# A fused FNet and GEGLU layer on one core: the opening of its pipeline in another order of instructions

## The chip, the core and the metric

The kernel runs on one core of a Trainium2 chip. The core has five engines with an instruction queue each: TensorE (PE in the profile, with its weight loads listed apart as PEld), VectorE (DVE), ScalarE (ACT), GpSimd (POOL) and SyncE (SP), which here only issues transfers. Each engine works through its own queue in order, and an instruction starts when what it waits for in other queues has come. The metric is the device time of one execution in microseconds (us); the median of three runs of the kernel before is 777.99 us.

## The reference, cut to what matters

`x` is 2048 rows by 448 columns. A normalised copy of it feeds two branches, and their product is added to `x`:

```
xn = layernorm(x)                                   # over the 448 columns
s  = dft_seq_re @ (xn @ dft_hid_re.T) - dft_seq_im @ (xn @ dft_hid_im.T)
g  = silu((gelu(xn @ w_gate) * (xn @ w_up)) @ w_down)   # w_gate, w_up 448x1792, w_down 1792x448
out = x + s * g
```

Everything is 32-bit. TensorE gets each operand as a rounded high part and a remainder, the low part; a product is high x high + high x low + low x high. So nearly every operand is made twice: ScalarE writes a high part (a copy to a rounded type), and VectorE or GpSimd subtracts it from the source to give the low part.

## The kernel before

The 2048 rows of `x` are four chunks c = 0 to 3 of 512 rows, each four tiles k of 128 rows. The 1792 columns of the two first weights are 14 blocks f of 128, in pairs; the work below on blocks 0 and 1 (the first pair) is the opening, some 75 us. After it come the other six pairs, in a Strassen form (`strassen`, L438 to L509) over two chunks at a time that needs differences of chunks and of weights; then the transforms. The first pair is done plainly so that TensorE has work while those differences are made.

The steps of the opening, with their lines before the change:

- `stats` gives four closures for a chunk. `one(i)` takes mean and variance of a tile (L155, L156, DVE). `root` takes a square root (L160, ACT) and two small terms (L161, L162); `newton` turns it into the reciprocal root in four DVE operations on 128 x 4 or 128 x 2 numbers (L166 to L170). `norm(i)` normalises a tile in place, on DVE in one operation (L178) or on ACT in two (L175, L176).
- `turn_mm` transposes a tile on TensorE into a PSUM bank (L187, two such banks in turn). `turn_split` then has ACT write the high part (L199) and one or two plain copies `xf` (L201), and DVE the low part (L202), in that order of writing.
- `prep_w` splits the raw weights of blocks 0 and 1: a high part, and a low part in two subtractions of 128 x 768 and 64 x 256 (L285, L287). Block 0 lies in `w`, block 1 in `wd`. In the kernel before GpSimd makes the low parts of block 0 and DVE those of block 1.
- `first` and `gu_mm` are the matmuls of gate and up (L556, L361). `act` runs the gelu of the gate on ACT (L386), and returns m (times up, DVE, L389), h (high part, ACT, L390) and l (low part, DVE, L391). ACT loads a table (ACT_TABLE_LOAD) when it goes from square root to gelu and back.
- `down_one` multiplies the result with the second weights (L415): for block 0 then block 1, the parts h, h and l, six matmuls in that order into one of two PSUM banks. ACT takes the result out (L422).
- `combine(p, s, eng)` are four subtractions of transposed tiles for a pair of chunks p and half s (L218, L222, L223, L224). The eight of chunks 0 and 1 are on DVE, put one by one between other steps (the list `comb`); the eight of chunks 2 and 3 are on GpSimd, and can start when the last copies of chunk 3 are there (GpSimd first clears a corner, L217).
- `prep_s` splits the weights of block 2 for the Strassen form, in two steps: ACT rounds (L321), DVE subtracts 128 x 512 and 64 x 384 in the first step and 128 x 896 in the second (L323, L327). `t_places` and `v_places` split the combined tiles (L143).

The scheduling is by hand (`tc.manual_schedule()`): each engine's queue is the order in which the Python code writes its instructions. `down` and `gateup` call closures from lists `between` and `between1` after each of their pieces, so that work of ACT and DVE falls between TensorE's.

Of the kernel before, what the change touches and what calls it, by code (L numbers as in the profile page):

```python
# [13 lines left out]
P = 128  # L14
# [31 lines left out]
def fnet_geglu(ctx: ExitStack, tc: tile.TileContext, x, ca, ct, cp, et, wgu, wd, out):  # L46
# [13 lines left out]
    nc = tc.nc  # L60
# [123 lines left out]
    def turn_mm(c, k):  # L184
        pt = tp_tile(f"pt{c}_{k}").rearrange("p (b d) -> p b d", b=4)
        for b in range(4):
            nc.tensor.transpose(pt[:, b], xr[c][:, k, b * P : (b + 1) * P], ident)  # L187
        return c, k, pt

    def turned(pt, c):  # L190
        return pt if c % 2 == 0 else pt.rearrange("p (b a) d -> p b a d", a=2)

    def cols_of(v, c, sl):
        return v[:, :, sl] if c % 2 == 0 else v[:, :, :, sl]

    def turn_split(c, k, pt):
        sl = slice(k * P, (k + 1) * P)
        h, l = [cols_of(xs(c, lo), c, sl) for lo in range(2)]
        nc.scalar.activation(h, turned(pt, c), AF.Copy)  # L199
        for i, v in enumerate(xf[c]):  # L200
            nc.scalar.activation(v[:, :, sl], pt[:, 3 * i :] if i else pt[:, : v.shape[1]], AF.Copy)  # L201
        nc.vector.tensor_sub(l, turned(pt, c), h)  # L202


    SPOT = ((0, 0), (1, 1), (1, 0), (0, 1))
# [310 lines left out]
    with tc.manual_schedule():  # L516
# [71 lines left out]
            nc.scalar.activation(xf[0][0][:, :, k * P : (k + 1) * P], t[2], AF.Copy)  # L588
        newton()
        norm(0)  # L590
        norm(1)
        ws[1][1](nc.vector)
        ws = [w[2] for w in ws]
        draw = load_d(GROUPS[0], a_r[0][:, 1024:])
        first(0, half[0], ("hh", "hl", "lh", "last"))
# [3 lines left out]
        one, root, newton, norm = stats(1, 0, 4)  # L599
        one(0)  # L600
        one(1)
        turn_split(*t2)
        turn_split(*t3)
        one(2)
        one(3)
        root()
# [8 lines left out]
        turn_split(*t0)  # L615
        turn_split(*t1)
# [4 lines left out]
        d_low()  # L621
# [5 lines left out]
        turn_split(*t2)  # L627
        turn_split(*t3)
        one(1)
        m0, h0, l0 = act(0, 0, pgs[0])  # L630
        m1, h1, l1 = act(1, 0, pgs[1])
        m0()
        h0()
        m1()
# [2 lines left out]
        one(3)  # L637
        root()
        l0()
        l1()  # L640
        newton()
        norm(0)
        norm(1)
        gu_mm(pg[0], ws[0], 0, 1, half[1], True)
        gu_mm(pg[1], ws[0], 1, 1, half[1])
        norm(2)
# [3 lines left out]
        pg = gu_ps(1, 1)  # L650
        for g in range(2):
            gu_mm(pg[g], ws[1], g, 1, slice(0, 512))
        turn_split(*turn_mm(2, 0))
        h0()
        xp = [dram.tile([P, 2, 1024], F32, name=f"xp{p}") for p in range(2)]

# [9 lines left out]
        spill(0)  # L666
        s_raw = load_s(GROUPS[1][0], 1)
        sums_s(s_raw, nc.gpsimd)
        comb = combine(0, 0, nc.vector) + combine(0, 1, nc.vector)

        def turn2(k):
            turn_split(*turn_mm(2, k))
            if k == 1:
                l0()
            comb.pop(0)()

        between = [lambda k=k: turn2(k) for k in (1, 2, 3)]
        down(0, 0, wdn, between)
# [1 line left out]
        one, root, newton, norm = stats(3, 0, 4)  # L680
        one(0)
        one(1)
        m1()
        h1()
        one(2)
        one(3)
        root()
        l1()
        newton()
        norm(0)  # L690
        norm(1)

        nws = [None, None]


        for c in (2, 3):
            if c == 2:
                draw = load_d(GROUPS[1], a_st[:, 2304:])
            else:
                s_raw2 = load_s(GROUPS[1][1], 1)  # L700
            m0, h0, l0 = gateup(0, c, ws[0])
            if c == 2:
                turn = lambda k: turn_split(*turn_mm(3, k))
                between = [
                    lambda: (m0(), h0(), norm(2)),
                    lambda: (l0(), norm(3), turn(0), comb.pop(0)()),
                    lambda: (turn(1), comb.pop(0)()),
                    lambda: (turn(2), comb.pop(0)()),
                ]
                between1 = [lambda: (turn(3), comb.pop(0)())]  # L710
            else:
                t_split = t_places(0)
                between = [
                    lambda: (m0(), v_split(2)),
                    lambda: (h0(), t_split(1)),
                    lambda: (l0(), t_split(2)),
                    lambda: (t_split(0), t_split(3)),
                ]
                between1 = [lambda: v_split(0), lambda: v_split(3)]
            down(0, c - 1, wdn, between)  # L720
            if c == 2:
                nws[0], steps = prep_s(0, s_raw)
                for f in steps:
                    f()
            m1, h1, l1 = gateup(1, c, ws[1], between1)
            m1()
            if c == 2:
                h1()
                l1()
                comb.pop(0)()  # L730
                v_split = v_places(0)
                v_split(1)
# [571 lines left out]
```

## Time and profile before

| | us |
|---|---|
| runs of the kernel before | 776.15, 777.99, 779.34 |
| median | 777.99 |
| profiled execution, its own time | 778.02 |
| span of the trace in it | 776.3 |
| granted TensorE clock over the span | 0.998 of full speed |

The profile is of one execution. A timeline row gives start, duration, engine, line and operation, tiles and shapes, and in brackets how long the engine stood idle before it and what ended that. Line numbers in rows are of the kernel before; in the changed file the same code stands 16 to 20 lines further down.

### The profile page before, as it was taken

What the parts mean: (1) busy time and instruction counts of PE and PEld (TensorE: products, weight loads), DVE (VectorE), ACT (ScalarE), POOL (GpSimd) and SP (SyncE); (2) the same over time, 40 slices, a digit from 0 to 9 for tenths busy, and PEclk for the clock granted to TensorE, in tenths of its full rate; (3) what the DMA queues carried; (4) which work ended last, traced back from release to release, by engine and by line L of the source; (5) the groups of instructions that cost most, each with busy time, mean ns of one, the idle gap of its engine ahead of it and who ended that gap; (6) DMA issues with size and microseconds to landing.
All of it is one profiled execution on the core that took longest, in us unless ns stands there. A gap on an engine that the chain in (4) does not pass through costs nothing.

```text
span 776.3 us, 11377 instructions
## 1 busy us (share of the span) xinstructions
PE 765.2 (99%) x4044; PEld 686.3 (88%) x4044; DVE 546.8 (70%) x937; ACT 363.6 (47%) x538; POOL 189.0 (24%) x308
## 2 busy tenths in 40 slices
PE   8999999999999999999999999999999999999997
PEld 7888888888888888888889999999999999899996
DVE  7789866555556555455553776988879696969687
ACT  3885545434434344344444685544344434434341
POOL 1109133330511512501011101223132231313120
PEclk9999999999999999999999999999999999999999
DMA  8232557994959968865979962869596969687784
GB/s 295 89 119 89 204 201 164 259 190 94 269 109 254 264 121 231 167 144 99 276 199 248 388 291 87 279 224 332 185 359 188 367 187 321 213 306 237 266 270 179
DMA packets 61370, 170.05 MB, mean 219 GB/s; under 512 B 7424, under 2 KB 40064, under 8 KB 60416
## 3 DMA queue, kind: packets, MB, share of 16 engines
q1 hardware_dynamic: 47440, 108.17, 39.4%
q0 software_dynamic: 13728, 61.02, 34.2%
q8 instruction: 32, 0.52, 0.3%
q14 instruction: 26, 0.21, 0.1%
q10 hardware_dynamic: 144, 0.11, 0.0%
HBM read 127.21 MB, written 70.91 MB: 255 GB/s over the span
## 4 chain that ended last, share of the span: by engine, by line
PE 83%; DVE 8%; DMA 5%; issue 2%; ACT 1%; SPq 0%; DVEq 0%; ACTq 0%
PE x L438 23%; PE po L415 17%; PE p L1111 16%; PE ab L927 9%; PE p L1114 8%; PE x L445 4%; PE gu L361 3%; DVE e L143 2%; DVE xt L143 1%; DMA raw<-wgu 1%; DMA raw_d<-ct 1%; DMA w<-td 1%; DMA raw<-ct 1%; DMA raw<-cp 1%; PE py L1126 1%
## 5 line engine op out<-in xcount | busy, mean ns | idle before, releaser
L438 PE MATMUL x<-xt,w 128*128 128x512 f32 x480 | 149.5, 392 | 0.0
L438 PEld LDWEIGHTS x<-xt,w 128*128 128x128 f32 x480 | 90.1, 188 | 16.1 <-DVE tmp L477 0.4
L422 ACT ACTIVATE po_out<-po 128x448 f32<-128x448 f32 x112 | 60.2, 538 | 82.1 <-PE po L415 81.2
L415 PE MATMUL po<-wd0h,hs 128*128 128x448 f32 x256 | 81.7, 366 | 0.0
L427 POOL DMA_DIRECT2D gs<-po_out x24 | 21.4, 890 | 219.3 <-ACT po_out L422 219.2
L927 PE MATMUL ab<-e,xt 128*128 128x448 f32 x288 | 68.8, 365 | 0.0
L415 PE MATMUL po<-wd,hs 128*128 128x448 f32 x288 | 66.0, 365 | 0.0
L438 PE MATMUL x<-t_v,w 128*128 128x512 f32 x216 | 60.7, 389 | 0.0
L415 PEld LDWEIGHTS po<-wd,hs 128*128 128x128 f32 x288 | 54.1, 188 | 6.7
L927 PEld LDWEIGHTS ab<-e,xt 128*128 128x128 f32 x288 | 54.1, 188 | 4.3
L415 PEld LDWEIGHTS po<-wd0h,hs 128*128 128x128 f32 x256 | 48.1, 188 | 5.0
L1006 POOL DMA_DIRECT2D raw<-sums x45 | 24.8, 551 | 98.4 <-DVE xt L143 30.6
L438 PEld LDWEIGHTS x<-t_v,w 128*128 128x128 f32 x216 | 40.5, 188 | 8.7
L415 PE MATMUL po<-wd0l,hs 128*128 128x448 f32 x128 | 46.9, 366 | 0.0
L142 ACT ACTIVATE e<-raw 128x896 fp32r<-128x896 f32 (+1 forms) x30 | 27.7, 922 | 34.3 <-DVE raw L1013 19.9
L493 ACT ACTIVATE hs<-tmp 128x512 fp32r<-128x512 f32 x24 | 15.2, 633 | 54.6 <-DVE tmp L491 54.6
L1111 PE MATMUL p<-t_v,wd0l 128*128 128x448 f32 x112 | 37.5, 380 | 2.8 <-DVE cc L1208 2.8
L438 PE MATMUL x<-t_lo,w 128*128 128x512 f32 x96 | 37.3, 389 | 0.0
L1006 POOL DMA_DIRECT2D tmp<-sums x39 | 21.4, 550 | 63.1 <-DVE xt L143 27.5
L1111 PE MATMUL p<-w,e 128*128 128x448 f32 x112 | 36.4, 374 | 0.0
L323 DVE TENSOR_TENSOR w<-raw,w 128x512 fp32r<-128x512 f32 (+1 forms) x24 | 21.3, 888 | 19.0 <-ACT w L321 19.0
L143 DVE TENSOR_TENSOR e<-raw,e 128x896 fp32r<-128x896 f32 (+1 forms) x30 | 31.4, 1046 | 4.4 <-ACT e L142 4.1
(317 smaller groups left out, 2015.5 us busy)
## 6 DMA issues: line engine op xcount, KB each, us to landing
gs<-po_out POOLq DMA_DIRECT2D x24, 896.0 KB, 8.3
sums<-ca SPq DMA_DIRECT2D x16, 896.0 KB, 9.8
sums<-ca POOLq DMA_DIRECT2D x16, 896.0 KB, 14.5
t_v<-td SPq DMA_DIRECT2D x24, 448.0 KB, 5.6
w<-td SPq DMA_DIRECT2D x24, 448.0 KB, 7.2
raw<-ct SPq DMA_DIRECT2D x45, 192.0 KB, 4.6
raw<-wgu SPq DMA_DIRECT2D x12, 640.0 KB, 5.7
tmp<-ct SPq DMA_DIRECT2D x39, 192.0 KB, 4.6
```

The costliest lines, as they stand in the source:

```text
L142: nc.scalar.activation(h, src, AF.Copy)
L143: nc.vector.tensor_sub(l, src, h)
L361: nc.tensor.matmul(ps[:, cols], a, xt[:, cols], start=n == 0, stop=n == len(mm) - 1)
L415: nc.tensor.matmul(po[:, :D], hs[:, a, kk * P : (kk + 1) * P], wdn[b][:, i], start=n == 0, stop=n == 5,)
L422: nc.scalar.activation(out_[0][:, kk], po[:, :D], AF.Copy)
L427: nc.gpsimd.dma_start(gv[:, 4 * c : 4 * c + 4], out_[0], accum_op=ALU.add)
L438: nc.tensor.matmul(ps, a[i], b[j], start=first and n == 0, stop=n == 2, skip_group_check=True)
L445: nc.tensor.matmul(ps, a[0], xt, start=False, stop=True, skip_group_check=True)
L927: nc.tensor.matmul(p[:, :D], a, b, start=n == 0, stop=n == len(mm) - 1)
L1006: nc.gpsimd.dma_start(v[:, 4 * P : 6 * P], sums[j][:, KS.index(k)])
L1111: nc.tensor.matmul(ps[q][:, :D], h, v, start=u % UN == 0, stop=False, skip_group_check=True)
L1114: nc.tensor.matmul(ps[q][:, :HD], l, v[:, :HD], start=False, stop=u % UN == NS - 1, skip_group_check=True,)
```

## The change

Seven edits, all in the opening:

1. `turn_split` takes several tiles. With two, it writes both high parts, then both low parts, then the copies; with one, the old order of low part after copies stays, unless `early` is set (set for tile 3 of chunk 2). `mid` is run between low parts and copies.
2. The second `norm` of tiles 2 and 3 of chunk 0 goes from DVE to ACT, and the low parts of block 1's weights go from DVE to GpSimd.
3. The gelus of chunk 0 (with their table load) are run ahead of the copies of chunk 1's last two tiles, and the low part of the second weights, `d_low`, after that pair's low parts.
4. l of block 1 (`l1`) of chunk 0 moves behind two norms of chunk 2.
5. Of the eight combinations of chunks 0 and 1, half 1 comes before half 0; the one at each tile of chunk 2 shrinks to one in all, and the others go to later places; three statistics of chunk 3 come before m of block 1, and l before the square root.
6. The gelu of block 0 of chunk 2, with its table load, moves from ahead of the second down to behind tile 2 of chunk 3; m, h and l with it.
7. The two steps of `prep_s` move from behind `down` (ahead of tile 3 of chunk 3) into the place between the two matmul groups of block 1: behind tile 3, between h, l of block 0.

```diff
+    def turn_split(*turns, mid=None, early=False):
+        hl = []
+        for c, k, pt in turns:
+            sl = slice(k * P, (k + 1) * P)
+            hl.append([cols_of(xs(c, lo), c, sl) for lo in range(2)])
+            nc.scalar.activation(hl[-1][0], turned(pt, c), AF.Copy)
+        def lows():
+            for (c, k, pt), (h, l) in zip(turns, hl):
+                nc.vector.tensor_sub(l, turned(pt, c), h)
+        early = early or len(turns) > 1
+        if early:
+            lows()
+        if mid:
+            mid()
+        for c, k, pt in turns:
...
+        if not early:
+            lows()
...
-        norm(1)
-        ws[1][1](nc.vector)
+        norm(1, nc.scalar)
+        ws[1][1](nc.gpsimd)
...
-        turn_split(*t2)
-        turn_split(*t3)
+        acts0 = []
+        turn_split(t2, t3, mid=lambda: acts0.extend(act(f, 0, pgs[f]) for f in range(2)))
+        d_low()
         one(1)
...
-        l1()
         newton()
         norm(0)
         norm(1)
+        l1()
...
-            turn_split(*turn_mm(2, k))
+            turn_split(turn_mm(2, k), early=k == 3)
             if k == 1:
                 l0()
-            comb.pop(0)()
+            if k == 1:
+                comb.pop(0)()
...
                 between = [
-                    lambda: (m0(), h0(), norm(2)),
-                    lambda: (l0(), norm(3), turn(0), comb.pop(0)()),
+                    lambda: norm(2),
+                    lambda: (norm(3), turn(0), comb.pop(0)()),
                     lambda: (turn(1), comb.pop(0)()),
-                    lambda: (turn(2), comb.pop(0)()),
+                    lambda: (turn(2), comb.pop(0)(), first.extend(act(0, 2, pg)), first[0]()),
                 ]
-                between1 = [lambda: (turn(3), comb.pop(0)())]
+                between1 = [lambda: (turn(3), first[1](), steps[0](), first[2](), steps[1]())]
...
                 nws[0], steps = prep_s(0, s_raw)
-                for f in steps:
-                    f()
             m1, h1, l1 = gateup(1, c, ws[1], between1)
             m1()
             if c == 2:
                 h1()
+                comb.pop(0)()
                 l1()
                 comb.pop(0)()
```

In VectorE's queue at the second statistics of chunk 0 (`sd_2`: two tiles) stood, before, the reciprocal root's steps, two norms, then the weights' low parts:

```order
L168 TENSOR_TENSOR sd_2_161<-sd_2_161 128x2
L169 TENSOR_TENSOR sd_2_161<-sd_2_161 128x2
L170 SCALAR_TENSOR_TENSOR sd_2_161<-sd_2_161 128x2
L178 TENSOR_SCALAR xr_a<-xr_a,mv_2_160,sd_2_161 128x512 x2
L285 TENSOR_TENSOR wd_78<-raw_75,wd_78 128x768
L287 TENSOR_TENSOR wd_78<-raw_75,wd_78 64x256
L155 BN_STATS st_0_237<-xf_71 128x6
```

After the change the two `wd` rows stand in GpSimd's queue, behind those of block 0 (`w`), with nothing between them:

```order
L301 TENSOR_TENSOR w<-raw_74,w 128x768
L303 TENSOR_TENSOR w<-raw_74,w 64x256
L301 TENSOR_TENSOR wd_78<-raw_75,wd_78 128x768
L303 TENSOR_TENSOR wd_78<-raw_75,wd_78 64x256
L319 TENSOR_TENSOR raw_75<-raw_75 128x128
```

VectorE's queue has lost three rows there, and GpSimd's has gained two whose input, the high part `wd`, ScalarE writes shortly before.

In VectorE's queue around the last tile of chunk 3 (`pt_3`, whose low part is `xt_69`) stood, before, the three subtractions of block 2's weights (`w<-raw_75`) ahead of that tile, and m of block 1 (the `tmp` row with `gu_2_1`) soon behind it:

```order
L222 TENSOR_TENSOR xf_72<-xf_72 128x512
L323 TENSOR_TENSOR w<-raw_75,w 128x512
L327 TENSOR_TENSOR w<-raw_75,w 64x384
L323 TENSOR_TENSOR w<-raw_75,w 128x896
L202 TENSOR_TENSOR xt_69<-pt_3_668,xt_69 128x2x2x128
L223 TENSOR_TENSOR xf_72<-xf_72 128x512
L389 TENSOR_TENSOR tmp<-tmp,gu_2_1_656 128x512
L391 TENSOR_TENSOR hs_79<-tmp,hs_79 128x512
```

After the change:

```order
L405 TENSOR_TENSOR tmp<-tmp,gu_2_1_558 128x512
L204 TENSOR_TENSOR xt_69<-pt_3_661,xt_69 128x2x2x128
L339 TENSOR_TENSOR w<-raw_75,w 128x512
L343 TENSOR_TENSOR w<-raw_75,w 64x384
L407 TENSOR_TENSOR hs_80<-tmp,hs_80 128x512
L339 TENSOR_TENSOR w<-raw_75,w 128x896
L405 TENSOR_TENSOR tmp<-tmp,gu_2_1_649 128x512
L238 TENSOR_TENSOR xf_72<-xf_72 128x512
L407 TENSOR_TENSOR hs_79<-tmp,hs_79 128x512
```

Between that tile's low part and m of block 1 now stand three weight subtractions and l of block 0 (`hs_80`), where one combination stood; and between m and l of block 1 (`hs_79`) one combination.

In ScalarE's queue there, before, ACT rounded the weights (`w<-raw_75`) ahead of that tile:

```order
L201 ACTIVATE po_out<-pt_2_640 128x128
L321 ACTIVATE w<-raw_75 128x896 x2
L199 ACTIVATE xt_69<-pt_3_668 128x2x2x128
L201 ACTIVATE raw_74<-pt_3_668 128x3x128
L201 ACTIVATE po_out<-pt_3_668 128x128
L386 ACTIVATE tmp<-gu_2_0_655 128x512
L390 ACTIVATE hs_79<-tmp 128x512
```

After the change:

```order
L214 ACTIVATE po_out<-pt_2_636 128x128
L402 ACT_TABLE_LOAD
L402 ACTIVATE tmp<-gu_2_0_557 128x512
L201 ACTIVATE xt_69<-pt_3_661 128x2x2x128
L214 ACTIVATE raw_74<-pt_3_661 128x3x128
L214 ACTIVATE po_out<-pt_3_661 128x128
L406 ACTIVATE hs_80<-tmp 128x512
L337 ACTIVATE w<-raw_75 128x896 x2
L402 ACTIVATE tmp<-gu_2_0_648 128x512
```

The last copies of chunk 3 (`po_out<-pt_3`), which let GpSimd's combinations start, now come ahead of the rounding of the weights instead of behind it.

## Rows read from the trace of the kernel before

**Rows 1.** The page's first part: busy time and share of the span by engine.
```profile
span 776.3 us, 11377 instructions
PE 765.2 (99%) x4044; PEld 686.3 (88%) x4044; DVE 546.8 (70%) x937; ACT 363.6 (47%) x538; POOL 189.0 (24%) x308
```

**Rows 2.** Chain of waits, 0 to 140 us: start, duration, what.
```profile
43.31 4.60 PE gu L361 x19
...
64.89 4.86 PE po L415 x24
```

**Rows 3.** Waits of TensorE's loads, 10 to 60 us: total, times, longest.
```profile
PEld gu L361 <- DVE xt L202: 1.5, 3, 0.8
PEld gu L556 <- DVE xt L202: 0.5, 1, 0.5
PEld pt L187 <- issue: 0.5, 1, 0.5
PEld pt L187 <- DVE xt L202: 0.4, 1, 0.4
PEld gu L556 <- DVE wd L285: 0.3, 1, 0.3
PEld gu L361 <- ACT xt L199: 0.2, 1, 0.2
```

**Rows 4.** Waits of VectorE, 10 to 60 us.
```profile
DVE xt L202 <- ACT xf L201: 3.7, 5, 1.5
```

**Rows 5.** Timeline, 8 to 15 us: chunk 0, tiles 2 and 3.
```profile
8.62 1.84 POOL L285 TENSOR_TENSOR w<-raw,w 128x768 fp32r<-128x768 f32 x1 [7.29 <-DVE w L282]
...
10.39 1.06 ACT L280 ACTIVATE wd<-raw 128x1024 fp32r<-128x1024 f32 x1 [1.80 <-DMA raw<-wgu]
...
10.53 0.74 POOL L287 TENSOR_TENSOR w<-raw,w 64x256 fp32r<-64x256 f32 x1
...
11.87 0.16 DVE L168 TENSOR_TENSOR sd<-sd 128x2 f32<-128x2 f32 x1
...
12.47 1.00 DVE L178 TENSOR_SCALAR xr_a<-xr_a,mv,sd 128x512 f32<-128x512 f32 x2
...
13.34 1.04 PE L187 MATMUL pt<-ident,xr_a 128*128 128x128 f32 x8
13.38 0.95 DVE L285 TENSOR_TENSOR wd<-raw,wd 128x768 fp32r<-128x768 f32 x1
```

**Rows 6.** Timeline, 36 to 38 us: m of block 0, chunk 1, and its PSUM bank's next use.
```profile
36.73 0.67 DVE L389 TENSOR_TENSOR tmp<-tmp,gu 128x512 f32<-128x512 f32 x1
...
37.46 0.47 PE L415 MATMUL po<-wd0h,hs 128*128 128x448 f32 x1
```

**Rows 7.** Timeline, 57 to 65 us: the last tile of chunk 3, and what follows.
```profile
57.15 0.68 DVE L323 TENSOR_TENSOR w<-raw,w 128x512 fp32r<-128x512 f32 x1
...
57.84 0.56 DVE L327 TENSOR_TENSOR w<-raw,w 64x384 fp32r<-64x384 f32 x1
...
58.26 0.36 ACT L201 ACTIVATE po_out<-pt 128x128 f32<-128x128 f32 x1
...
58.43 1.09 DVE L323 TENSOR_TENSOR w<-raw,w 128x896 fp32r<-128x896 f32 x1
...
59.27 1.40 POOL L218 TENSOR_TENSOR xf<-raw,xf 128x512 f32<-128x512 f32 x1
...
60.75 1.62 POOL L222 TENSOR_TENSOR raw<-po_out,raw 128x512 f32<-128x512 f32 x1
61.15 0.67 DVE L389 TENSOR_TENSOR tmp<-tmp,gu 128x512 f32<-128x512 f32 x1
61.85 0.63 ACT L390 ACTIVATE hs<-tmp 128x512 fp32r<-128x512 f32 x1 [2.75 <-DVE tmp L389]
...
62.52 1.77 DVE L391 TENSOR_TENSOR hs<-tmp,hs 128x512 fp32r<-128x512 f32 x1 [0.70 <-ACT hs L390]
...
64.73 0.36 PE L415 MATMUL po<-wd0h,hs 128*128 128x448 f32 x1
```

More of the change, by code (lines that the diff above doesn't have):

```diff
@@ L194, in cols_of @@
         return v[:, :, sl] if c % 2 == 0 else v[:, :, :, sl]
[L196 to L202, printed above, removed]
+    def turn_split(*turns, mid=None, early=False):
[13 more added lines that the diff above has]
+        for c, k, pt in turns:
+            sl = slice(k * P, (k + 1) * P)
+            for i, v in enumerate(xf[c]):
+                nc.scalar.activation(
+                    v[:, :, sl], pt[:, 3 * i :] if i else pt[:, : v.shape[1]], AF.Copy
+                )
+        if not early:
+            lows()
     SPOT = ((0, 0), (1, 1), (1, 0), (0, 1))
@@ L601, in fnet_geglu @@
         one(1)
-        turn_split(*t2)
-        turn_split(*t3)
+        turn_split(t2, t3)
         one(2)
@@ L614, in fnet_geglu @@
         first(1, half[1], ("lh", "last"))
-        turn_split(*t0)
-        turn_split(*t1)
+        turn_split(t0, t1)
         one, root, newton, norm = stats(2, 0, 4)
@@ L626, in fnet_geglu @@
         gu_mm(pg[1], ws[0], 1, 1, half[0])
-        turn_split(*t2)
-        turn_split(*t3)
+        acts0 = []
+        turn_split(t2, t3, mid=lambda: acts0.extend(act(f, 0, pgs[f]) for f in range(2)))
+        d_low()
         one(1)
-        m0, h0, l0 = act(0, 0, pgs[0])
-        m1, h1, l1 = act(1, 0, pgs[1])
+        (m0, h0, l0), (m1, h1, l1) = acts0
         m0()
@@ L652, in fnet_geglu @@
             gu_mm(pg[g], ws[1], g, 1, slice(0, 512))
-        turn_split(*turn_mm(2, 0))
+        turn_split(turn_mm(2, 0))
         h0()
@@ L668, in fnet_geglu @@
         sums_s(s_raw, nc.gpsimd)
-        comb = combine(0, 0, nc.vector) + combine(0, 1, nc.vector)
+        comb = combine(0, 1, nc.vector) + combine(0, 0, nc.vector)
         def turn2(k):
-            turn_split(*turn_mm(2, k))
+            turn_split(turn_mm(2, k), early=k == 3)
             if k == 1:
                 l0()
-            comb.pop(0)()
+            if k == 1:
+                comb.pop(0)()
         between = [lambda k=k: turn2(k) for k in (1, 2, 3)]
@@ L682, in fnet_geglu @@
         one(1)
+        one(2)
         m1()
         h1()
-        one(2)
         one(3)
+        l1()
         root()
-        l1()
         newton()
@@ L700, in fnet_geglu @@
                 s_raw2 = load_s(GROUPS[1][1], 1)
-            m0, h0, l0 = gateup(0, c, ws[0])
             if c == 2:
-                turn = lambda k: turn_split(*turn_mm(3, k))
+                pg = gu_ps(0, c)
+                for g in range(2):
+                    gu_mm(pg[g], ws[0], g, c, slice(0, 512))
+                first = []
+            else:
+                m0, h0, l0 = gateup(0, c, ws[0])
+            if c == 2:
+                turn = lambda k: turn_split(turn_mm(3, k))
                 between = [
-                    lambda: (m0(), h0(), norm(2)),
-                    lambda: (l0(), norm(3), turn(0), comb.pop(0)()),
+                    lambda: norm(2),
+                    lambda: (norm(3), turn(0), comb.pop(0)()),
                     lambda: (turn(1), comb.pop(0)()),
-                    lambda: (turn(2), comb.pop(0)()),
+                    lambda: (turn(2), comb.pop(0)(), first.extend(act(0, 2, pg)), first[0]()),
                 ]
-                between1 = [lambda: (turn(3), comb.pop(0)())]
+                between1 = [lambda: (turn(3), first[1](), steps[0](), first[2](), steps[1]())]
             else:
@@ L713, in fnet_geglu @@
                 between = [
-                    lambda: (m0(), v_split(2)),
+                    lambda: (m0(), v_split(2), comb.pop(0)()),
                     lambda: (h0(), t_split(1)),
@@ L728, in fnet_geglu @@
                 h1()
+                comb.pop(0)()
                 l1()
```

1 line of the change is left out of this document (removed).

## The prediction

> **What bounds the kernel now.** I read the page's first part first: TensorE is busy 99% of the span, VectorE 70%, ScalarE 47%, GpSimd 24% [rows 1]. So an engine other than TensorE matters only where TensorE stands still for it, and a change can win no more than those stops. Then the chain of waits: from 43.31 us it runs through TensorE's matmuls without a break to the end of the opening, as the row of 24 matmuls at 64.89 shows [rows 2]; in front of that it goes back and forth between TensorE, VectorE and ScalarE. Third, the waits of TensorE's weight loads from 10 to 60 us, because a load stops together with its matmul and shows the stop more fully: 1.5 + 0.5 + 0.5 + 0.4 + 0.3 + 0.2 = 3.4 us, in eight stops [rows 3]. All but one wait for a low part or a normalised tile of VectorE; one waits 0.2 for ScalarE. That is the whole prize, 0.4% of the time. Measured runs of this kernel can tell a difference of about 0.5%, 3.9 us, from no change; so I count "faster" below 774.1 and "slower" above 781.9.
>
> **The low parts ahead of the copies (edits 1 and 3).** VectorE stood 3.7 us, in five waits, not for the high part that the subtraction needs but for the copy that ScalarE makes after it [rows 4]. With both low parts ahead of both copies that wait goes, and the low parts of a pair come sooner by up to the longest of the five, 1.5. Together with the lighter VectorE (edits 2 and 5: two subtractions of 0.95 and 0.4, one norm and, at chunk 2, two combinations gone from the places where TensorE waits) this is more than any single stop of rows 3, the longest of which is 0.8. I take all 3.4 as gone. What is late next is in the following three terms; the price of the copies being later is rival 3.
>
> **Term a: GpSimd takes over weights' low parts (edit 2).** In the row, ScalarE has the high part of block 1 ready at 10.39 + 1.06 = 11.45; GpSimd is free by 11.3 (10.53 + 0.74) and would subtract from 11.5 to 13.35 (1.84, as for block 0) and then another 0.74, to about 14.2 [rows 5]. The sum is in time for its own user: TensorE asks for those low parts after the transposes, at 14.4. But VectorE's root steps (11.87 and after) and the norm of tile 2 (12.47) now run at the same time. In rows 7, a VectorE subtraction of 128 x 512 with both inputs in SBUF takes 1.77 while GpSimd subtracts, where the same shape took 0.68 at 57.15, before GpSimd began: it is not slowed evenly but held until GpSimd's instruction is over (62.52 + 1.77 = 64.29). If only the norm is held, it ends at 13.35 + 0.5 = 13.85, half of the row's 1.00 being one norm, and the transposes start there instead of at 13.34: 0.5. If the narrow root steps are held too, the first waits until 13.35, the second behind GpSimd's second subtraction until 14.2, the norm ends at about 15.1: 1.8. If nothing is held, nothing is lost. So 0 to 1.8. The rows of an operation of the same kind are the held ones, so I take a value near the upper end, 1.5.
>
> The Trainium skill, "SBUF — State Buffer", section "Who interferes with whom", says that a VectorE instruction with two SBUF inputs contends with a GpSimd instruction that reads SBUF, and that whichever starts first has the port for its whole instruction. Rows 7 agree for wide tiles, 1.77 against 0.68; no row here shows a narrow one. By that rule the term would be the full 1.8 and the sum 0.3 higher.
>
> **Term b: m of block 0, chunk 1.** The second output bank of `down` is the one that this m reads. Before, m ends at 36.73 + 0.67 = 37.40 and TensorE's first matmul into that bank starts at 37.46 [rows 6]: no slack. The stops ahead of that place are all of rows 3 but the last two (0.8 and 0.4), 2.2; less term a, TensorE comes there 0.7 sooner. The same VectorE work, four norms and l of block 1, still stands ahead of m. If m comes no sooner, that costs 0.7; if as much sooner, nothing. I take 0.4.
>
> **Term c: the weights of block 2 meet GpSimd's combinations (edits 6 and 7).** This is the large one. Before, the three weight subtractions ran on VectorE one after the other at their own pace, 0.68, 0.56 and 1.09, and ended at 59.52, just as GpSimd's combinations began at 59.27 [rows 7]. Now ScalarE makes the last copies of chunk 3 first, and these let GpSimd start; the weights come behind. I count from the end of that last copy (58.26 + 0.36 = 58.62 before). GpSimd's first combination starts 59.27 - 58.62 = 0.65 later and is over at 2.05 (1.40). ScalarE's h of block 0 (0.63) and one rounding of 896 columns (at most the 1.06 of the 1024 columns in rows 5) put VectorE's first weight subtraction at 1.7 at the latest, so it finds GpSimd at work and is held to 2.05. Each further one finds the next combination (eight stand in a row) and is held 1.77 - 0.68 = 1.1. So: first subtraction to 2.05 + 0.68 = 2.7; second (64 x 384) to 2.7 + 1.1 + 0.56 = 4.4; l of block 0 to 4.4 + 1.77 = 6.2; third (128 x 896) to 6.2 + 1.1 + 1.09 = 8.4. Then m of block 1, which reads PSUM and took 0.67 beside GpSimd, to 9.0, and its h on ScalarE (0.63) to 9.7.
>
> TensorE wants that h as the fourth matmul of the next `down`. Its first came 64.73 - 58.62 = 6.1 after the copy, and the matmuls between are the same; at 4.86 / 24 = 0.2 each [rows 2] the fourth comes at 6.7. So TensorE stops for 9.7 - 6.7 = 3.0. It wants l as the sixth, 0.4 behind the fourth, at 10.1. VectorE has put a combination ahead of l: it is held by what is left of GpSimd's fifth (some 0.5), to 10.1, and l is held again, to 10.1 + 1.77 = 11.9: another 1.8. That makes 4.8; each hold may begin with GpSimd's instruction partly done, so I take 4.6. Bounds: nothing, if VectorE is not held (it would then reach h at 0.63 + 1.06 + 0.68 + 0.56 + 0.68 + 1.09 + 0.67 + 0.63 = 6.0, in time), and 5.5 if the hold on the widest grows with it.
>
> Edit 4, the statistics of edit 5 and the transfers: no transfer is added, and SyncE's queue keeps its order. Nothing else here is waited for within a microsecond, so I count it as nothing, covered by TensorE's matmuls; the covered part is l of block 1 (0.7) if its cover goes.
>
> **Sum.** The profiled execution took 778.02, against a median of 777.99, so no correction between them is needed. 778.0 - 3.4 + 1.5 + 0.4 + 4.6 = 781.1. What is lost at term c is not won back, since TensorE has no stops behind it to lose: after 43.31 the chain is its own.
>
> **Rivals.** (1) The narrow root steps are not held: term a is 0.5, and the time 778.0 - 3.4 + 0.5 + 0.4 + 4.6 = 780.1. For it: no row shows such an operation held. Against: same engine, same opcode, both inputs in SBUF.
>
> (2) Faster: VectorE gets its weight subtractions in before or between GpSimd's combinations without being held, term c is nothing, and the time is 778.0 - 3.4 + 1.5 + 0.4 = 776.5, or 775.5 with term a at 0.5. It decides at GpSimd's first combination: it would have to start some 5 us behind the last copy, not 0.65, or m of block 1 be done within 6 us of that copy. For it: VectorE reaches the place with less behind it, having done two combinations less. Against: the hold of rows 7, and that both queues are in order.
>
> (3) ScalarE becomes the late one. The copies of three pairs now wait for two low parts (0.68 each), and behind them stand a square root, the rounding of the second weights and a gelu with its table load. If two of the three cost TensorE 0.6 each, the time is 782.3. For it: gelu and table load stand ahead of two copies that free the transposes' banks. Against: ScalarE is busy 47% [rows 1].
>
> **Numbers.** Forecast 0.45, rival 1 0.25, rival 2 0.20, rival 3 0.10. The forecast's own range is 780.0 to 782.3: term c down by 1, or b, a and c up by 0.3 each. For eight in ten I go from 775.6 to 782.5: it takes in rival 1, most of rival 3 and all but the lower part of rival 2. Above 781.9 lie a fifth of the forecast and most of rival 3, some tail besides: 0.20. Below 774.1 only a rival 2 with no price at all: 0.06. The rest, 0.74, is within 0.5%.
>
> **What would show it.** In the new profile, if term c is right: TensorE stops in the `down` of chunk 2 for ScalarE's h (about 3) and then for VectorE's l (about 1.8), at some 65 to 70 us, with the weight subtractions there at 1.5 to 2.5 each beside GpSimd's combinations. If term a is right: a stop of 1 to 2 us at the transposes after 13.3 us, with a root step or norm of VectorE ending together with GpSimd's subtraction. If the removed stops are right: nothing above 0.2 for low parts between 16 and 33 us and at the first gate matmuls of chunk 2. VectorE's weight subtractions at 0.6 to 1.1 each would make the whole forecast wrong, toward rival 2; a stop whose cause is a copy of ScalarE speaks for rival 3.

## The result, and the profile after

| | kernel before | changed kernel |
|---|---|---|
| median of 14 runs, us | 778.78 (776.15 to 781.37) | 782.77 (779.36 to 787.6) |
| ratio to before, 95% interval | | 1.0043 (1.0024 to 1.0061) |
| profiled execution, us; its span | 778.02; 776.3 | 781.69; 779.8 |

The change costs 0.43%, inside the half per cent that was given 0.74. The forecast's ratio is 781.1 / 778.0 = 1.0040. The median of 782.77 lies 0.3 over the upper end of the range, but the kernel before, run beside it, was 0.8 over its own earlier median; on that earlier footing the ratio puts the changed kernel at 781.3.

The page's first part, as in [rows 1]: TensorE is still the bound, and GpSimd has gained.

```profile
PE 766.5 (98%) x4044; PEld 687.9 (88%) x4044; DVE 547.9 (70%) x934; ACT 365.5 (47%) x540; POOL 193.4 (25%) x310
```

The waits of TensorE's weight loads, 10 to 130 us of the changed kernel (line, what it waited for, us in total, times, longest). These answer to [rows 3]:

```profile
PEld po L431 <- ACT hs L406: 2.6, 1, 2.6
PEld pt L187 <- ACT xr_a L176: 1.7, 1, 1.7
PEld po L431 <- DVE hs L407: 1.6, 1, 1.6
PEld x L454 <- DVE tmp L493: 0.4, 1, 0.4
PEld gu L572 <- DVE xt L598: 0.4, 1, 0.4
PEld po L431 <- DVE tmp L405: 0.2, 1, 0.2
```

None of the six waits of [rows 3] is left, and three long ones are new. The one of 1.7 is at the transposes of chunk 0's last two tiles. Timeline of the changed kernel there (start, length, engine and line, operation, in brackets the idle time ahead and what ended it), against [rows 5]:

```profile
11.80 1.84 POOL L301 TENSOR_TENSOR wd<-raw,wd 128x768 fp32r<-128x768 f32 x1 [0.27 <-POOL w L303]
...
12.09 1.57 DVE L168 TENSOR_TENSOR sd<-sd 128x2 f32<-128x2 f32 x1
...
13.72 0.73 POOL L303 TENSOR_TENSOR wd<-raw,wd 64x256 fp32r<-64x256 f32 x1
13.89 0.58 DVE L170 SCALAR_TENSOR_TENSOR sd<-sd 128x2 f32<-128x2 f32 x1
14.51 0.55 DVE L178 TENSOR_SCALAR xr_a<-xr_a,mv,sd 128x512 f32<-128x512 f32 x1
14.56 0.72 ACT L176 ACTIVATE xr_a<-xr_a,sd 128x512 f32<-128x512 f32 x1 [1.13 <-DVE sd L170]
...
15.31 0.96 PE L187 MATMUL pt<-ident,xr_a 128*128 128x128 f32 x7 [1.55 <-ACT xr_a L176]
```

A root step of two numbers per partition takes 1.57 instead of 0.16, and ends at 13.66 where GpSimd's subtraction ends at 13.64. Two steps on, L170 takes 0.58 instead of 0.16 beside GpSimd's second piece. ScalarE's second norm pass, which needs the root, comes last, and TensorE behind it.

The other two long waits are in the second product on chunk 2, against [rows 7]:

```profile
56.89 0.29 ACT L214 ACTIVATE po_out<-pt 128x128 f32<-128x128 f32 x1
...
57.84 1.30 POOL L234 TENSOR_TENSOR xf<-raw,xf 128x512 f32<-128x512 f32 x1
...
58.57 1.11 DVE L339 TENSOR_TENSOR w<-raw,w 128x512 fp32r<-128x512 f32 x1 [0.66 <-ACT w L337]
59.22 1.62 POOL L238 TENSOR_TENSOR raw<-po_out,raw 128x512 f32<-128x512 f32 x1
...
59.70 1.55 DVE L343 TENSOR_TENSOR w<-raw,w 64x384 fp32r<-64x384 f32 x1
...
61.28 1.67 DVE L407 TENSOR_TENSOR hs<-tmp,hs 128x512 fp32r<-128x512 f32 x1
62.48 1.62 POOL L240 TENSOR_TENSOR xf<-xf,po_out 64x512 f32<-64x512 f32 x1
62.88 2.17 DVE L339 TENSOR_TENSOR w<-raw,w 128x896 fp32r<-128x896 f32 x1
63.33 0.36 PE L431 MATMUL po<-wd0h,hs 128*128 128x448 f32 x1
...
64.97 0.67 DVE L405 TENSOR_TENSOR tmp<-tmp,gu 128x512 f32<-128x512 f32 x1
65.57 1.15 DVE L238 TENSOR_TENSOR xf<-xf 128x512 f32<-128x512 f32 x1
65.68 0.63 ACT L406 ACTIVATE hs<-tmp 128x512 fp32r<-128x512 f32 x1 [5.81 <-DVE tmp L405]
...
66.36 0.74 PE L431 MATMUL po<-wd0h,hs 128*128 128x448 f32 x1 [2.26 <-ACT hs L406]
66.65 1.76 DVE L407 TENSOR_TENSOR hs<-tmp,hs 128x512 fp32r<-128x512 f32 x1
...
68.46 0.74 PE L431 MATMUL po<-wd0h,hs 128*128 128x448 f32 x1 [0.98 <-DVE hs L407]
```

VectorE and GpSimd take turns. VectorE's four instructions from 59.70 (two subtractions, l of block 0 and m, L405) took to 65.6. TensorE began the product at 63.33, which is 1.40 earlier than before (64.73, [rows 7]; the 64.89 of [rows 2] is a row of the chain of waits, which dates the same matmul 0.16 later); it needs h of block 1 three matmuls later and gets it at 66.3.

The last two matmuls of TensorE in these rows take 0.74, where one of the same form takes 0.36 at 63.33. The windows show why. After the stretch and its length come busy time and count of PE, PEld, DVE, ACT and POOL, then the granted clock, as a share of 2.4 GHz, and last the transfers (busy share of the DMA engines, GB/s). The changed kernel:

```profile
66.00:73.40 7.40, 6.05 (x16) 4.90 (x17) 7.40 (x7) 3.92 (x8) 7.17 (x8) 0.54 0.24 89
```

and the kernel before in the same stretch:

```profile
66.00:73.40 7.40, 7.40 (x36) 6.48 (x35) 7.40 (x6) 6.69 (x13) 7.17 (x6) 1.00 0.24 99
```

It is 1.00 in the changed kernel from 60 to 66 us and again from 73.4 to 80. Behind the two stops the clock was at its lower level (1.2 GHz) for most of 7.4 us, and TensorE did 16 matmuls there instead of 36. This was in no term of the sum.

To tell what the opening costs apart from the rest, take one place late enough: the second run of 24 matmuls in block 2, a row of the chain of waits. First the changed kernel, with the 19 matmuls behind the second stop; then the kernel before.

```profile
68.46 6.28 PE po L431 x19
...
91.01 5.46 PE x L454 x24
```

```profile
86.06 5.46 PE x L438 x24
```

The changed kernel is 4.95 late there, and matmul for matmul it stays so (within 0.02) until 545 us. Its span is only 3.5 longer. The other 1.4 was given back in the last stage, where the code is the same. About half of it is TensorE's: its last matmul is 4.26 late (775.01 against 770.75), for TensorE waits there for VectorE's combinations of results, and waited less. The rest was given back behind that matmul, where VectorE's combinations end the span. TensorE's waits for them from 130 us on, before and after:

```profile
PEld p L1111 <- DVE cc L1208: 4.4, 6, 1.2
```

```profile
PEld p L1131 <- DVE cc L1228: 3.5, 5, 1.2
```

They change from profile to profile, between 2.7 and 6.1 in the fourteen seen here, so they are probably a good part of the scatter of the times, which no run singles out. I therefore give two numbers for each experiment: the ratio of times with its interval, and the lateness of that run of 24 matmuls against 86.06, from one profile. Two profiles of one kernel differed by 0.41 in the second.

### The profile page after: what moved, and what is told of

It reads as the page before. It is cut to its first block, busy times and chain, and to the rows that moved or that the text cites. A ratio compares the mean times of both kernels' runs of the same rounds, so it can differ in the third digit from the quotient of the medians.

```text
span 779.8 us, 11370 instructions
## 1 busy us (share of the span) xinstructions
PE 766.5 (98%) x4044; PEld 687.9 (88%) x4044; DVE 547.9 (70%) x934; ACT 365.5 (47%) x540; POOL 193.4 (25%) x310
## 4 chain that ended last, share of the span: by engine, by line
PE 74%; DVE 9%; DMA 8%; issue 5%; ACT 1%; POOL 1%; SPq 0%; DVEq 0%; POOLq 0%; ACTq 0%
PE x L454 23%; PE po L431 17%; PE p L1131 10%; PE ab L947 9%; PE p L1134 5%; PE x L461 4%; PE gu L377 3%; DMA raw<-sums 2%; DMA tmp<-sums 2%; DVE xt L143 2%; DVE e L143 2%; DMA raw<-wgu 1%; DMA tmp<-ct 1%; DMA raw_d<-ct 1%; PE gu L572 1%
## 5 line engine op out<-in xcount | busy, mean ns | idle before, releaser
L431 PE MATMUL po<-wd0h,hs 128*128 128x448 f32 x256 | 84.0, 375 | 3.2 <-ACT hs L406 2.3
```

The lines of the kernel that those rows point to most:

```text
L431: nc.tensor.matmul(po[:, :D], hs[:, a, kk * P : (kk + 1) * P], wdn[b][:, i], start=n == 0, stop=n == 5,)
```

## The experiments

Each ran in five rounds beside the kernel before. All but two are edits of the changed kernel.

**1. Edit 7 undone.**

```diff
-                between1 = [lambda: (turn(3), first[1](), steps[0](), first[2](), steps[1]())]
+                between1 = [lambda: (turn(3), first[1](), first[2]())]
...
                 nws[0], steps = prep_s(0, s_raw)
+                for f in steps:
+                    f()
```

> The changed kernel with edit 7 undone: block 2's weight subtractions stand behind the second product's groups again, as in the kernel before. Theory (the subtractions and GpSimd's combinations hold each other, TensorE stops 2.3 + 1.0 us near 63 to 68 us, and its granted clock of 0.54 in 66.0 to 73.4 is the consequence of these stops): both stops go, the granted clock of 66 to 73.4 us is 1.00, and 3.8 us of stops and 2.6 us of slow clock go, less up to 1 us of new stops where the subtractions now stand: 5.4 to 6.4 us less than the changed kernel, ratio to the kernel before 0.996 to 0.9975. Rival 1 (the stops come from ScalarE's order, the gelus ahead of the copies, and not from the subtractions): within 1 us of the changed kernel, ratio 1.003 to 1.0055, with the stops at the same matmuls. Rival 2 (the clock falls there whatever stops): only 3 to 4 us less, ratio 0.999 to 1.0005, and the granted clock near 66 to 73 us stays under 0.7.

Measured: ratio 0.9984 (0.9965 to 1.0003); granted clock 1.00 from 60 to 80 us; the run of 24 at 86.36. The two new waits of 10 to 130 us:

```profile
PEld gu L377 <- DVE xt L204: 1.2, 1, 1.2
PEld x L454 <- DVE tmp L405: 0.9, 1, 0.9
```

It is late by 0.30: undoing edit 7 takes away 4.65 of the 4.95. That is less than the theory's 5.4, and the ratio a little above its 0.9975, because these two waits came in place of the others. The stops at the second product are gone, which speaks against rival 1, and the clock stays up without them, against rival 2.

**2. Edit 2 undone** (norm of tile 3 and block 1's low parts back on VectorE).

```diff
-        norm(1, nc.scalar)
-        ws[1][1](nc.gpsimd)
+        norm(1)
+        ws[1][1](nc.vector)
```

> The changed kernel with edit 2 undone: the third and fourth tile's norm and block 1's weight low parts on VectorE again. Theory (GpSimd's low part held VectorE's 128x2 root step 1.57 us, and TensorE waited 1.7 us for ScalarE's second norm pass behind it): the root step is back near 0.16 us and the 1.7 us stop at 15 us goes; block 1's low parts then stand in VectorE's row and give back up to 1 us of the small stops that the change removed: 0.7 to 1.7 us less than the changed kernel, ratio to the kernel before 1.002 to 1.0035. Rival (the wait ended by ScalarE, which now normalises two tiles, is what costs, and VectorE's work takes as long): within 0.4 us of the changed kernel, ratio about 1.004.

Measured: ratio 1.0053 (1.0032 to 1.0073), which the intervals don't tell from the changed kernel's 1.0043; the run of 24 at 91.26, late by 5.20. Timeline rows:

```profile
12.18 0.17 DVE L168 TENSOR_TENSOR sd<-sd 128x2 f32<-128x2 f32 x1
...
17.93 1.46 PE L572 MATMUL gu<-xt,w 128*128 128x256 f32 x10 [0.33 <-DVE xt L204]
...
21.43 0.74 PE L187 MATMUL pt<-ident,xf 128*128 128x128 f32 x5 [0.61 <-ACT xf L176]
```

The cause of term a is shown: without GpSimd beside it the root step takes 0.17, and the stop of 1.7 at the transposes is gone. But the theory's gain did not come. VectorE now does the 1.4 us of subtractions itself, and small stops came back: 0.33 and 0.61 in these rows, and at the weight loads 0.8, 0.5, 0.2 and 0.2, which is 1.7 again. The second product on chunk 2 begins at 63.27, against 63.33 with the edit. Its two stops (2.29 and 1.37) and the low clock (0.56 from 66 to 73.4 us) are there as in the changed kernel.

**3. Edits 2 and 7 undone** (both diffs above).

> The changed kernel with edits 2 and 7 both undone. Theory (the two costs lie at different places and add): the sum of the two single runs, 6 to 8 us less than the changed kernel, ratio to the kernel before 0.994 to 0.997; what is left of the change is then the removed stops of rows 3, worth 3.4 us. Rival (the removed stops are not worth 3.4 us, since TensorE catches up with later waits): ratio 0.998 to 1.000.

Measured: ratio 1.0005 (0.9985 to 1.0026); the run of 24 at 85.88, early by 0.18. The theory was wrong in adding the two. With edit 7 out, undoing edit 2 as well moves the opening by 0.48 (86.36 to 85.88), hardly more than two profiles of one kernel differ, and the time no way that shows; and edits 1, 3, 4, 5 and 6 together are worth nothing that shows. The waits of 1.2 and 0.9 of experiment 1 are here too.

**4. TensorE kept busy in the stops**: 18 further matmuls, unused, in its row.

```diff
                 n += 1
+                if (gi, c, kk) == (0, 2, 0) and n in (3, 5):
+                    t = tp_tile(f"fill{n}")
+                    for _ in range({3: 12, 5: 6}[n]):
+                        nc.tensor.matmul(
+                            t[:, :D], hs_of[0, 2][:, 0, :P], wdn[0][:, 0],
+                            start=True, stop=True, skip_group_check=True,
+                        )
```

> The changed kernel whole, with 18 more matmuls (12 behind the third, 6 behind the fifth matmul of block 0's second product on chunk 2, into a spare bank, their result unused) that stand in TensorE's row where it stops 2.3 and 1.0 us. Theory (the granted clock of 0.54 in 66.0 to 73.4 us follows from these stops): with the stops filled the granted clock there is 1.00, the added matmuls lie in the wait (18 x 0.2 us = 3.7 us beside 3.3 us of stops), and the time falls by 1.8 to 2.6 us, ratio to the kernel before 1.000 to 1.0025. Rival (the clock falls there for another reason): the granted clock stays near 0.54, the added matmuls run at 0.37 us each, and the time is 0 to 4 us more than the changed kernel's, ratio 1.004 to 1.010.

Measured: ratio 1.0010 (0.9992 to 1.0027). A window row, and the rows of the chain that answer to 68.46 and 91.01:

```profile
66.00:73.40 7.40, 7.13 (x35) 5.95 (x34) 7.40 (x7) 3.84 (x8) 7.17 (x7) 1.00 0.27 89
```

```profile
68.62 4.19 PE po L431 x19
...
89.13 5.46 PE x L461 x24
```

VectorE and ScalarE deliver h and l when they did before, and the 19 matmuls begin 0.16 later than without the fill; but they take 4.19 instead of 6.28. So the low clock followed from TensorE's standing still, and cost 2.09 us. The theory's 2.6 was a little high: of the slow stretch, the part ahead of 68.46 was hidden by the wait for l.

**5. GpSimd's combinations of chunks 2 and 3 left out**, so that the later stages of this kernel work on uncombined tiles.

```diff
-                    for f in combine(1, 1, nc.gpsimd) + combine(1, 0, nc.gpsimd):
-                        f()
```

> The changed kernel whole, but without GpSimd's eight combination instructions of chunks 2 and 3 (pair 1 is left uncombined, so the second half of the work goes on with uncombined tiles). Theory (VectorE's subtractions are long because GpSimd's combinations run beside them, not because VectorE's row is full): the subtractions that took 1.55, 1.67 and 2.17 us take 0.56, 0.69 and 1.09 us, neither stop of 2.3 and 1.0 us is there though edit 7 is in, the granted clock is 1.00 at 66 to 73 us, and the time falls by 5 to 7 us against the changed kernel: ratio to the kernel before 0.9955 to 0.998. Rival (edits 6 and 7 put more into VectorE's row than it can do before TensorE comes, GpSimd or not): a stop of 1.5 us or more stays at the third matmul of the second product, ratio 1.000 or more.

Measured: ratio 0.9998 (0.9985 to 1.0011), clock 1.00 from 60 to 80 us; the run of 24 at 84.77. Timeline rows:

```profile
59.39 0.56 DVE L343 TENSOR_TENSOR w<-raw,w 64x384 fp32r<-64x384 f32 x1
59.98 0.69 DVE L407 TENSOR_TENSOR hs<-tmp,hs 128x512 fp32r<-128x512 f32 x1
60.59 1.08 DVE L339 TENSOR_TENSOR w<-raw,w 128x896 fp32r<-128x896 f32 x1
61.59 0.68 DVE L405 TENSOR_TENSOR tmp<-tmp,gu 128x512 f32<-128x512 f32 x1
...
63.45 0.36 PE L431 MATMUL po<-wd0h,hs 128*128 128x448 f32 x1
```

With edits 6 and 7 both in and only GpSimd quiet, the subtractions take 0.56, 0.69 and 1.08 as the theory said, m ends 3.4 earlier than in the changed kernel, and neither stop is there. The opening is 6.24 shorter than the changed kernel's and 1.29 shorter than before's. The time fell by less, 0.45% or 3.5 us; in this profile the waits of the last stage are 4.9 against the changed kernel's 3.5. The ratio is above the theory's range, the mechanism is not in doubt.

**6. Edit 7 alone**, on the kernel before.

```diff
-                    between1 = [lambda: (turn(3), comb.pop(0)())]
+                    between1 = [lambda: (turn(3), comb.pop(0)(), steps[0](), steps[1]())]
...
-                for f in steps:
-                    f()
```

> The kernel before with edit 7 alone: block 2's weight subtractions stand behind chunk 3's last turn, inside block 1's matmul groups. Theory (the subtractions beside GpSimd's combinations are enough, the six other edits have no part in it): the stops of the changed kernel appear here too, 2.3 to 2.6 us and 1.0 to 1.6 us before the second product on chunk 2, the granted clock behind them falls under 0.7, and the 0.8 us that the subtractions cost at their old place go: 4.5 to 6 us more than the kernel before, ratio 1.0055 to 1.008. Rival (edit 7 is harmless alone and costs only together with the later gelu of edit 6): within 1 us of the kernel before, ratio 0.9985 to 1.0015, clock 1.00.

Measured: ratio 1.0033 (1.0016 to 1.0050); the run of 24 at 89.00, late by 2.94. Window and timeline:

```profile
66.00:73.40 7.40, 5.58 (x25) 4.71 (x26) 6.70 (x6) 4.17 (x8) 7.17 (x6) 1.00 0.26 89
```

```profile
66.83 0.47 PE L415 MATMUL po<-wd0h,hs 128*128 128x448 f32 x1 [1.04 <-ACT hs L390]
...
68.49 0.68 PE L415 MATMUL po<-wd0h,hs 128*128 128x448 f32 x2 [0.99 <-DVE hs L391]
```

Edit 7 is enough to make stops at the same two matmuls, so this rival falls; but the first is 1.04 and not 2.26, and the clock stays up. The theory had both wrong: it had taken the size from the changed kernel, where edit 6 puts l of block 0 (1.67) among the subtractions. Count from the end of the last copy of chunk 3, which is at 57.18 in the changed kernel and at 58.84 here. TensorE begins the product 6.15 and 6.19 behind it, but h of block 1 is ready 9.13 behind it there and 7.94 here. Alone, edit 7 costs the opening 2.94; taken out of the changed kernel it gave back 4.65.

**7. Edit 6 undone**, edit 7 kept: gelu, m, h and l of block 0 on chunk 2 at their old places.

```diff
...
-                    lambda: (turn(2), comb.pop(0)(), first.extend(act(0, 2, pg)), first[0]()),
+                    lambda: (turn(2), comb.pop(0)()),
...
-                between1 = [lambda: (turn(3), first[1](), steps[0](), first[2](), steps[1]())]
+                between1 = [lambda: (turn(3), steps[0](), steps[1]())]
```

> The changed kernel with edit 6 alone undone: gelu, h and l of block 0 on chunk 2 where they stood before, edit 7 kept. Theory (edit 7 makes the stops, edit 6 lengthens the first by the one held instruction that it puts between the subtractions, l of block 0, 1.67 us; and only the longer stop is followed by the low clock): the first stop is 0.6 to 1.1 us, the second stays at 1.0 us or more, the granted clock is 1.00 at 66 to 73 us, 3 to 4.5 us less than the changed kernel, ratio 0.9985 to 1.0005. Rival (edit 6 has no part in the stop): both stops as in the changed kernel, granted clock near 0.5 behind them, ratio 1.003 to 1.0055.

Measured: ratio 1.0031 (1.0013 to 1.0049); the run of 24 at 89.73, late by 3.67. Window and timeline:

```profile
66.00:73.40 7.40, 5.96 (x22) 5.08 (x22) 7.40 (x7) 3.92 (x9) 7.16 (x6) 0.77 0.20 79
```

```profile
65.74 0.47 PE L431 MATMUL po<-wd0h,hs 128*128 128x448 f32 x1 [0.53 <-ACT hs L406]
...
67.85 1.12 PE L431 MATMUL po<-wd0h,hs 128*128 128x448 f32 x2 [1.44 <-DVE hs L407]
```

The first stop shrinks to 0.53 (0.9 at its weight load), as the theory said: l of block 0 (1.67 when held) no longer stands ahead of m. Counted from the last copy (58.26) as in experiment 6, h of block 1 is ready after 7.43, which is 1.70 sooner than in the changed kernel. But the second stop grows to 1.44, and behind it the clock fell all the same, for a shorter time: the 19 matmuls took 5.58. So the theory was wrong on the clock, and its range of the ratio too low by that; the ratio lies in the rival's range, though the rival, which left the first stop as it was, is not borne out. Over these runs the clock fell behind idle stops of 2.26 and 0.98, of 2.29 and 1.37 (experiment 2), and of 0.53 and 1.44, and did not behind 1.04 and 0.99. More than that these runs don't tell.

**8. Edit 1 alone**, on the kernel before: pairs of tiles through the new `turn_split`, all else as it was. The diff shows one of three such places.

```diff
...
-        turn_split(*t2)
-        turn_split(*t3)
+        turn_split(t2, t3)
```

> The kernel before with edit 1 alone: the low parts of two turned tiles ahead of the tiles' copies, in all places where tiles are turned in pairs. Theory (rows 3's waits for VectorE's low parts, 1.5 + 0.5 + 0.4 us, are the copies' doing): they go, 1.5 to 2.4 us less, ratio 0.997 to 0.998. Rival (the copies are only put off, and delay ScalarE's gelus and VectorE's low part of the second weights behind them, so a new stop of 1 to 1.6 us comes near 35 to 38 us, which edits 3 and 4 are there for): -1 to +0.5 us, ratio 0.9985 to 1.0005.

Measured: ratio 1.0012 (0.9996 to 1.0029); the run of 24 at 86.80, late by 0.74. Timeline:

```profile
29.80 5.29 PE L377 MATMUL gu<-xt,wd 128*128 128x512 f32 x22 [0.50 <-ACT tmp L402]
35.90 0.30 PE L187 MATMUL pt<-ident,xr_a 128*128 128x128 f32 x1 [0.80 <-issue]
```

The rival was right in that edit 1 alone doesn't pay, but the ratio is above its range too, and its cause is only part of the loss. The waits for low parts of [rows 3] near 24 and 28 us went, and TensorE begins the 22 matmuls on block 1 0.57 earlier than before (29.80 against 30.37), held up only by a gelu behind the copies that were put off. The stop at 35.90 stands in the profile without a releaser; the transpose needs VectorE's norms, which begin at 35.16 against 34.61 before. Of these 0.55, 0.15 come with the gelus. The other 0.40 is once more a meeting with GpSimd, which begins its sums of block 2's weights at 34.21 instead of 35.41: two root steps of VectorE take 0.35 and 0.39 where they take 0.17 before.

```profile
34.35 0.35 DVE L169 TENSOR_TENSOR sd<-sd 128x4 f32<-128x4 f32 x1
...
34.73 0.39 DVE L170 SCALAR_TENSOR_TENSOR sd<-sd 128x4 f32<-128x4 f32 x1
```

With edits 3, 4 and 5 beside it edit 1 pays (experiment 9); which of the three it needs, no run tells.

**9. Edits 1 to 5 in two forms, and the subtractions moved the other way.** The first kernel has edits 1, 3, 4 and 5, with 2, 6 and 7 undone as in the diffs above; it ran in two sittings. The second has edit 2 besides. The third is the changed kernel with edit 2 undone and the subtractions ahead of GpSimd's combinations instead of among them:

```diff
...
-                    lambda: norm(2),
+                    lambda: (norm(2), steps[0]()),
...
-                    lambda: (turn(1), comb.pop(0)()),
+                    lambda: (turn(1), steps[1](), comb.pop(0)()),
```

> The changed kernel with edits 2, 6 and 7 undone, so that of the change edits 1, 3, 4 and 5 are left. Theory (edit 7 cost the 3.3 us of stops and 2.6 us of slow clock, edit 2 some 0.5 us, edit 6 the 0.9 us stop before block 2 that both runs without edit 7 showed near 78 us): none of these is there, the stop near 58 us is 0.7 us or less, and what the remaining edits save of rows 3 shows: 1 to 2.5 us less than the kernel before, ratio 0.9965 to 0.9985. Rival (the stops that the edits take away come back elsewhere, VectorE's row being full up to 80 us): ratio 0.9995 to 1.001.

> Edits 1, 3, 4 and 5 again, beside the run of edits 1 to 5 on the same chip. Theory: a ratio near the first sitting's 0.9981, between 0.997 and 0.999, and so faster than both kernels. Rival (the first sitting was chance): 0.9995 to 1.001.

> The changed kernel with edits 6 and 7 undone, edit 2 kept: edits 1 to 5. Theory (edit 2 costs 1.55 to 1.8 us at the third turn and takes away only 0.33 + 0.6 us further on): 0.5 to 0.8 us more than the run with edits 1, 3, 4 and 5, which here would be hidden by the scatter: ratio 0.998 to 0.9995. Rival (edit 2 is a gain once the stops near 65 us are gone): 0.5 us or more below that run, ratio 0.997 or less.

> The changed kernel with edit 2 undone and block 2's weight subtractions moved ahead, to the third norm and the second turn of chunk 3, where GpSimd combines nothing; edit 6 stays. Theory (it is the meeting with GpSimd and not the place in TensorE's row that costs): no stop over 0.7 us between 40 and 72 us and a granted clock of 1.00; 0.5 to 2.5 us less than the kernel before, ratio 0.9965 to 0.9995. Rival (VectorE's row is full there, so the subtractions delay the turns' low parts): a new stop of 1 to 2 us near 50 us, ratio 1.000 to 1.002.

| kernel | ratio, interval | run of 24 | against 86.06 |
|---|---|---|---|
| edits 1, 3, 4, 5 | 0.9981 (0.9966 to 0.9996) | 85.61 | -0.45 |
| the same again | 0.9990 (0.9972 to 1.0007) | 85.20 | -0.86 |
| edits 1 to 5 | 0.9990 (0.9968 to 1.0013) | 85.44 | -0.62 |
| edits 1, 3 to 6, subtractions early | 0.9996 (0.9978 to 1.0014) | 85.58 | -0.48 |

All four have the granted clock of 1.00 in 66 to 73.4 us, and TensorE no wait over 0.8 between 20 and 130 us. Edits 1, 3, 4 and 5 come out ahead of both kernels, by 0.8 to 1.5 us against the one before; the interval of the second sitting alone would allow none. Edit 2 moves the opening by no more than two profiles of one kernel differ, so neither the theory (0.5 to 0.8 more) nor its rival is shown. Edit 6 without edit 7 costs the opening 0.92 beside edit 2 (86.36 in experiment 1, 85.44 with edits 1 to 5) and 0.27 to 0.68 without it (85.88 in experiment 3, against 85.61 and 85.20); the times don't show it. Moved ahead of GpSimd, the subtractions make no stop that long: it is the meeting that costs, and not the distance from the old place. The gain is not clear of the scatter, with a ratio just above the theory's range.

## Why the prediction was nearly right, and where it was not

The forecast was likeliest, and its mechanism is the one found: the subtractions of block 2, sent among GpSimd's combinations. Step by step, against what the profile and the runs gave:

| term | forecast | measured |
|---|---|---|
| stops removed | -3.4 | -3.3 (the rest of the sum; all six rows gone) |
| a, GpSimd's low part of block 1 | +1.5 (0 to 1.8) | +1.7 |
| b, m and the second output bank | +0.4 | +0.2 (the wait for `tmp`) |
| these three, at the first matmul of the second product on chunk 2 | -1.5 | -1.40 |
| c, subtractions among combinations | +4.6 (0 to 5.5) | +4.2 in stops (2.6 and 1.6) |
| clock behind the stops of c | none | +2.1 |
| opening | +3.1 | +4.95 |

**Term a** was right in kind and 0.2 short. I had taken 1.5, since no row showed a narrow instruction held. It was held for as long as GpSimd's instruction ran. The Trainium skill, "SBUF — State Buffer", section "Who interferes with whom", gave the full 1.8 by its rule, in which whoever comes first keeps the port for its whole instruction; the 1.57 of the root step, over at 13.66 beside GpSimd's 13.64, agrees, and experiment 2 takes it away with its cause. Rival 1, root steps not held, is refuted.

**Term c** was worked out as 3.0 for h and 1.8 for l and cut to 4.6; the weight loads waited 2.6 and 1.6. Its steps were right one by one: counted from the last copy, GpSimd's first combination ends at 1.96 (worked out: 2.05), h of block 1 is ready at 9.13 (9.7) and l at 11.23 (11.9). Experiments 1 and 5 show both sides of it: take away edit 7, or GpSimd's part, and the two stops are gone. Rival 2, no hold, is refuted by rows of 1.55, 1.67 and 2.17 that take 0.56, 0.69 and 1.08 alone.

**The step that failed** is that the sum prices a stop of TensorE at its own length: what the clock does behind a stop has no term, and no reason is given for leaving it out. The granted clock was 0.54 over 7.4 us, and the 19 matmuls there cost 2.09 more (experiment 4). That makes the opening 1.85 worse than forecast: 2.1 for the clock and 0.1 for the first three terms, less the 0.4 of term c.

The last sentence of the sum failed too, that what is lost at term c is not won back since TensorE has no stops left behind 43 us. It has some 4 us of them in the last stage, outside the stretch from 10 to 60 us that I read, and the span there ends with VectorE and not with TensorE. In the profiled execution 1.4 was given back there. So it is luck that the time was hit so closely: the two errors nearly cancel, and without the second the forecast would have been some 2 us short. Whether a late opening makes those waits shorter as a rule stays open: of the five kernels that were late by 2.9 or more, all have a ratio that is 0.4 to 2.3 us better than their opening, but their intervals are some 1.5 us to either side.

**Rival 3**, ScalarE late, is not seen: ScalarE's instructions ahead of the long waits had themselves waited for VectorE (1.13 and 5.81 in the rows above). The delay that it feared, a gelu late behind copies, shows where edit 1 stands alone (0.50, experiment 8).

**Two readings were loose**, though nothing hangs on them. One of the rows of [rows 3], 0.5, names no releaser, and I counted it as VectorE's. And the forecast's own range, 780.0 to 782.3, is a little wider than its two moves give: 780.1 with term c down by 1, 782.0 with three terms up by 0.3.

**What the -3.4 is made of** I had not seen. I credited it to edits 1, 2, 3 and 5 by their local savings. The runs show that edit 1 alone loses 0.74, edit 2 only exchanges stops, and edit 6 without edit 7 costs 0.3 to 0.9 of the opening. What stays is worth 0.8 to 1.5 in the time. My reading, which no run tests by itself, is that the stops of [rows 3] are mostly VectorE's nearly full row (43 of the 50 us from 10 to 60 in the kernel before) and come back at the next place where TensorE asks it for something.

## What to carry to other kernels

- Before moving a subtraction of two SBUF tensors on VectorE, look at what GpSimd does at the new place. Four instructions that take 3.0 alone took 5.9 there; the same subtractions placed some 8 us earlier, where GpSimd combined nothing, took 0.69, 0.56 and 1.08 and made no long stop.
- A stop of TensorE has to be priced with the granted clock behind it: here 2.1 us on top of 4.2. And one edit can lengthen the stop that another makes: l of block 0, put by edit 6 among the held subtractions, was held for 1.67 itself.
- When several edits each remove small stops of one engine that is nearly full, sum the engine's work up to the next place where it is waited for, and not the stops.

## What was not expected of the hardware

- VectorE's instruction on 128 x 2 elements was held by GpSimd for 1.57, just as the wide ones are; alone it takes 0.16 to 0.17. The reciprocal ahead of it, which has one input, began at 11.88 beside the same GpSimd instruction and took 0.17.
- Two stops of 2.26 and 0.98, between stretches in which TensorE was busy without a break, were followed by the lower clock for most of 7.4 us; 1.04 and 0.99 were not. Filling the stops with unused matmuls kept the clock at 1.00 and brought the run of 24 matmuls 1.88 forward (91.01 to 89.13), though it did not shorten the wait itself; the ratio fell from 1.0043 to 1.0010, with intervals that just overlap.
